# Two MLPs behind window attention: the first MLP's activation as Relu and Square on ScalarE and one max/min on VectorE

## The chip, the cores and the metric

One core of one Trainium2 chip. The time is the device time of one execution in microseconds; three executions of the kernel before took 999.17, 999.47 and 1000.1 us, median 999.47. Engines by the profile's names: PE is TensorE (PEld its weight loads), DVE VectorE, ACT ScalarE, POOL GpSimd, SP SyncE, which issues the DMAs.

## What is computed

Attention with a window of 128 keys over 4 batches, 8 heads, 576 positions and heads of 64 columns, then two MLPs on the 2304 tokens of 512 columns, each with 2048 hidden columns:

```python
h = x @ w_in                                  # first MLP
neg = h <= -1.0
pos = h >= 1.0
g = np.where(pos, h, np.where(neg, 0.0, (h + 1.0) ** 2 / 4.0))
x = g @ w_out
h = x @ w_in2                                 # second MLP
g = h * np.clip(h + 3.0, 0.0, 6.0) / 6.0
out = g @ w_out2
```

## The kernel before

All products keep fp32 accuracy: an operand is split into a high part in fp32r and the rest, and a product is three matmuls (low times high, high times low, high times high).

The tokens of the first MLP come in seven blocks: three of 256 and four of 384. A block runs over 16 chunks of the hidden columns (f). Per chunk, `first` (L549) makes h in one PSUM bank with twelve matmuls; `activate` (L578 to L580) makes r from it, ScalarE casts r to the high part of g (L137), GpSimd subtracts for the low part (L144; VectorE in the last block), and two chunks later `second` (L591) multiplies g by w_out with twelve matmuls. h alternates between two banks in the first three blocks and in the last one; in the blocks between, from the first wide one on, it has one bank (`h0`), so that the next chunk's matmuls wait until L580 has read h.

In the kernel before, the activation is max(h, square(min(max(h, -1), 1)/2 + 1/2)):

- L578, VectorE: r = min(max(h, -1), 1), h from PSUM
- L579, ScalarE: r = Square(0.5 r + 0.5)
- L580, VectorE: r = max(h, r), h from PSUM again

Attention is run in between. For each head and block of queries there is a step: scores on TensorE (L329), bias and row minimum on VectorE (L350), Exp on ScalarE (L353), for most heads a sum, reciprocal and scaling (L356, L357 on VectorE, L358 on GpSimd), transposes on TensorE (L380, L381), their split (L137 ScalarE, L393 VectorE) and the product with v (L466, or L411 in the first units). L303 and L305 split k, L141 casts v on whichever engine the scheduler picks (`nc.any`). A hook after each chunk issues attention's steps and the conversion of the weights of w_in and w_out, which arrive as fp64 words (L178 and L179 on ScalarE, L185 to L189 on VectorE, then a split by L137 and L144, operations of 128 x 1024).

The last block of the first MLP has no attention beside it; there the second MLP's weights are converted (names with `wb`, `mb`, `rawb`). The second MLP activates with L635 (ScalarE, Relu from PSUM, immediately scaled and biased) and L636 (VectorE, min and multiply in one operation).

The order on each engine is not the program's: the framework's scheduler simulates the program with its own costs and orders every engine's instructions by it (except SP's, which keep the program's order). An engine runs its instructions strictly in that order. So other operations in `activate` give another order around them.

Of the kernel before, what the change touches and what calls it, by code (L numbers as in the profile page):

```python
# [14 lines left out]
AF = mybir.ActivationFunctionType  # L15
ALU = mybir.AluOpType
# [22 lines left out]
def tile_window_attention_two_mlps(  # L39
# [15 lines left out]
    nc = tc.nc  # L55
# [7 lines left out]
    scale = 1.0 / math.sqrt(D)  # L63
# [71 lines left out]
    def split_hi(eng, hi, x):  # L135
        if eng == "act":
            nc.scalar.copy(hi, x)  # L137
        elif eng == "pool":
            nc.gpsimd.tensor_scalar(out=hi, in0=x, scalar1=1.0, scalar2=1.0, op0=ALU.mult, op1=ALU.mult)
        else:  # L140
            engines[eng].tensor_copy(hi, x)  # L141

    def split_lo(eng, lo, x, hi):
        engines[eng].tensor_tensor(out=lo, in0=x, in1=hi.bitcast(F32), op=ALU.subtract)  # L144
# [417 lines left out]
    class Mlp1(Mlp):  # L562
# [11 lines left out]
        def activate(self, ps, n):  # L574


            r, g = self.tiles()
            nc.vector.tensor_scalar(out=r[:, :n], in0=ps[:, :n], scalar1=-1.0, scalar2=1.0, op0=ALU.max, op1=ALU.min)  # L578
            nc.scalar.activation(out=r[:, :n], in_=r[:, :n], func=AF.Square, bias=0.5, scale=0.5)  # L579
            nc.vector.tensor_tensor(out=r[:, :n], in0=ps[:, :n], in1=r[:, :n], op=ALU.max)  # L580
            split_hi(HI["g"], g[:, 0, :n], r[:, :n])
            split_lo(LO[self.g_lo], g[:, 1, :n], r[:, :n], g[:, 0, :n])
            return g
# [305 lines left out]
```

## Time and profile before

| | |
|---|---|
| median of three executions | 999.47 us |
| span of the profiled execution | 997.9 us |
| execution time around that span | not recorded apart; the three executions lie 1.3 to 2.2 us above it |
| PE, PEld busy | 968.9, 882.8 us |
| DVE, ACT, POOL busy | 602.9, 515.9, 259.3 us |
| instructions on DVE, ACT, POOL | 1544, 1260, 403 |

The span goes from the first to the last instruction on the chip. TensorE is busy 97% of it, and its granted clock is 0.85 of full speed from 25 to 50 us and 1.00 from 50 us on. The first 50 us are loads and attention alone, then attention and the first MLP run together to about 525 us, the first MLP's last block to about 600, and the second MLP to the end.

### The profile page before, as it was taken

What the parts mean: (1) busy time and instruction counts of PE and PEld (TensorE: products, weight loads), DVE (VectorE), ACT (ScalarE), POOL (GpSimd) and SP (SyncE); (2) the same over time, 40 slices, a digit from 0 to 9 for tenths busy, and PEclk for the clock granted to TensorE, in tenths of its full rate; (3) what the DMA queues carried; (4) which work ended last, traced back from release to release, by engine and by line L of the source; (5) the groups of instructions that cost most, each with busy time, mean ns of one, the idle gap of its engine ahead of it and who ended that gap; (6) DMA issues with size and microseconds to landing.
All of it is one profiled execution on the core that took longest, in us unless ns stands there. A gap on an engine that the chain in (4) does not pass through costs nothing.

```text
span 997.9 us, 16828 instructions
## 1 busy us (share of the span) xinstructions
PE 968.9 (97%) x5748; PEld 882.8 (88%) x5748; DVE 602.9 (60%) x1544; ACT 515.9 (52%) x1260; POOL 259.3 (26%) x403
## 2 busy tenths in 40 slices
PE   7799999999999999999999999999999999999998
PEld 5687888999999998899999999999988888888886
DVE  4889996587678666668764998942242224223222
ACT  5688874567657566656653878522242223222121
POOL 3335454456545555455530000000000000000000
PEclk9899999999999999999999999999999999999999
DMA  5685823223212121222203884000030002001001
GB/s 171 168 258 173 271 66 87 78 67 94 75 42 80 50 80 44 63 59 80 62 12 105 293 277 169 1 1 1 1 106 1 1 1 84 1 1 43 1 1 42
DMA packets 75092, 80.00 MB, mean 80 GB/s; under 512 B 8704, under 2 KB 67072, under 8 KB 75008
## 3 DMA queue, kind: packets, MB, share of 16 engines
q1 hardware_dynamic: 75008, 78.94, 25.8%
q8 instruction: 45, 0.74, 0.3%
q14 instruction: 39, 0.32, 0.1%
HBM read 68.42 MB, written 10.49 MB: 79 GB/s over the span
## 4 chain that ended last, share of the span: by engine, by line
PE 85%; DVE 6%; ACT 4%; issue 2%; DMA 2%; POOL 1%; SPq 0%; ACTq 0%; DVEq 0%; POOLq 0%
PE h L549 37%; PE acc L646 20%; PE acc L591 17%; PE s L329 3%; PE r L466 3%; PE r L411 2%; PE t L380 1%; PE t L381 1%; DVE kl L305 1%; DVE r L578 1%; DMA qr<-qT 1%; ACT p L353 1%; DVE r L580 1%; DVE p L350 1%; DMA vr<-v 1%
## 5 line engine op out<-in xcount | busy, mean ns | idle before, releaser
L549 PE MATMUL h<-x,wa 128*128 128x384 f32 (+1 forms) x1344 | 231.5, 316 | 4.4 <-DVE r L580 2.5
L591 PE MATMUL acc<-g,wa 128*128 128x384 f32 (+1 forms) x1344 | 228.8, 315 | 1.7 <-POOL g L144 1.5
L549 PEld LDWEIGHTS h<-x,wa 128*128 128x128 f32 x1344 | 207.6, 190 | 7.0 <-DVE r L580 4.4
L549 PE MATMUL h<-x,wb 128*128 128x512 f32 (+1 forms) x960 | 210.5, 368 | 0.0
L591 PEld LDWEIGHTS acc<-g,wa 128*128 128x128 f32 x1344 | 206.3, 189 | 4.0 <-POOL g L144 2.2
L646 PE MATMUL acc<-wb,g 128*128 128x512 f32 x864 | 209.4, 390 | 0.0
L549 PEld LDWEIGHTS h<-x,wb 128*128 128x128 f32 x960 | 176.3, 188 | 25.0
L646 PEld LDWEIGHTS acc<-wb,g 128*128 128x128 f32 x864 | 161.7, 188 | 32.3
L636 DVE SCALAR_TENSOR_TENSOR r<-r,h 128x512 f32<-128x512 f32 (+1 forms) x80 | 50.7, 633 | 195.5 <-ACT r L635 195.4
L635 ACT ACTIVATE r<-h 128x512 f32<-128x512 f32 (+1 forms) x80 | 44.4, 556 | 207.9 <-PE h L549 207.8
L137 ACT CAST g<-r 128x384 fp32r<-128x384 f32 (+2 forms) x192 | 98.3, 512 | 69.6 <-DVE r L636 48.7
L144 POOL TENSOR_TENSOR g<-r,g 128x256 fp32r<-128x256 f32 (+1 forms) x96 | 92.0, 958 | 129.2 <-ACT g L137 114.0
L579 ACT ACTIVATE r<-r 128x384 f32<-128x384 f32 (+1 forms) x112 | 53.6, 478 | 93.5 <-DVE r L578 93.3
L353 ACT ACTIVATE p<-p,sm 128x256 f32<-128x256 f32 (+2 forms) x160 | 76.0, 476 | 24.4 <-DVE sm L350 21.6
L144 DVE TENSOR_TENSOR g<-r,g 128x384 fp32r<-128x384 f32 (+1 forms) x96 | 59.9, 624 | 44.7 <-ACT g L137 44.6
L578 DVE TENSOR_SCALAR r<-h 128x384 f32<-128x384 f32 (+1 forms) x112 | 55.5, 496 | 37.4 <-PE h L549 33.2
L144 POOL TENSOR_TENSOR qs<-qr,qs 64x256 fp32r<-64x256 f32 (+3 forms) x88 | 68.8, 781 | 28.4 <-issue 7.5
L580 DVE TENSOR_TENSOR r<-h,r 128x384 f32<-128x384 f32 (+1 forms) x112 | 55.7, 497 | 28.9 <-ACT r L579 28.3
L350 DVE CUSTOM_DVE_ANT_0 p<-s,dist 128x256 f32<-128x256 f32 (+2 forms) x160 | 59.7, 375 | 11.1 <-PE s L329 8.8
L358 POOL TENSOR_SCALAR p<-p,sm 128x256 f32<-128x256 f32 (+1 forms) x104 | 48.1, 463 | 61.7 <-DVE sm L357 37.4
L329 PE MATMUL s<-kh,qs 128*128 128x256 f32 (+2 forms) x160 | 55.0, 347 | 1.8 <-POOL qs L144 1.2
L305 DVE SCALAR_TENSOR_TENSOR kl<-kr,kh 128x256 fp32r<-128x256 f32 (+4 forms) x88 | 51.7, 587 | 7.3 <-ACT kh L303 7.1
(75 smaller groups left out, 1153.5 us busy)
## 6 DMA issues: line engine op xcount, KB each, us to landing
rawa<-w_in SPq DMA_DIRECT2D x16, 512.0 KB, 5.6
rawa<-w_out SPq DMA_DIRECT2D x16, 512.0 KB, 5.1
rawb<-w_in SPq DMA_DIRECT2D x16, 512.0 KB, 3.8
rawb<-w_out SPq DMA_DIRECT2D x16, 512.0 KB, 4.6
kr<-kT SPq DMA_DIRECT2D x80, 64.0 KB, 2.3
out<-o SPq DMA_DIRECT2D x18, 256.0 KB, 2.1
qr<-qT SPq DMA_DIRECT2D x64, 64.0 KB, 2.3
vr<-v SPq DMA_DIRECT2D x24, 128.0 KB, 2.4
```

The source lines that it names most:

```text
L137: nc.scalar.copy(hi, x)
L144: engines[eng].tensor_tensor(out=lo, in0=x, in1=hi.bitcast(F32), op=ALU.subtract)
L305: nc.vector.scalar_tensor_tensor(out=u.kl[:, :nk], in0=u.kr[:, :nk], scalar=unit, in1=u.kh[:, :nk].bitcast(F32), op0=ALU.mult, op1=ALU.sub ...
L329: nc.tensor.matmul(ps[:m, :nk], q[:, qo:qo + m], k[:, ko:ko + nk], start=(w == 0), stop=(w == len(parts) - 1))
L350: nc.vector.tensor_tensor_reduce(out=pt[:m, :nk], in0=ps[:m, :nk], in1=dist[:m, bo:bo + nk], scale=-slopes[u.h], scalar=3.0e38, op0=ALU.ad ...
L353: nc.scalar.activation(out=pt[:m, :nk], in_=pt[:m, :nk], func=AF.Exp, bias=sm[:m, 0:1], scale=-1.0, accum_out=None if u.whole else sm[:m, ...
L549: nc.tensor.matmul(ps[:, :n], self.W.w_in(a, c, f), self.x_chunk(x, b, c, n), start=(k == 0), stop=(k == 3 * KC - 1))
L578: nc.vector.tensor_scalar(out=r[:, :n], in0=ps[:, :n], scalar1=-1.0, scalar2=1.0, op0=ALU.max, op1=ALU.min)
L579: nc.scalar.activation(out=r[:, :n], in_=r[:, :n], func=AF.Square, bias=0.5, scale=0.5)
L580: nc.vector.tensor_tensor(out=r[:, :n], in0=ps[:, :n], in1=r[:, :n], op=ALU.max)
L591: nc.tensor.matmul(acc[i][:, o * n:(o + 1) * n], self.W.w_out(a, f)[:, e * P:(e + 1) * P], g[:, b, :n], start=(first and k == 0 and o == 0 ...
L646: nc.tensor.matmul(acc[t][:, :DM], g[:, b, t * P:(t + 1) * P], self.W.w_out(a, f), start=(first and k == 0), stop=(last and k == 2))
```

## The change

The activation is computed as min(max(h, 1), square(relu(h/2 + 1/2))). For h >= 1 the square is at least h, so the minimum is h; for h <= -1 the Relu gives 0; between, the square is at most 1. Relu from PSUM and Square are ScalarE operations, maximum and minimum are one VectorE operation with two inputs.

```diff
             r, g = self.tiles()
-            nc.vector.tensor_scalar(out=r[:, :n], in0=ps[:, :n], scalar1=-1.0, scalar2=1.0, op0=ALU.max, op1=ALU.min)
-            nc.scalar.activation(out=r[:, :n], in_=r[:, :n], func=AF.Square, bias=0.5, scale=0.5)
-            nc.vector.tensor_tensor(out=r[:, :n], in0=ps[:, :n], in1=r[:, :n], op=ALU.max)
+            nc.scalar.activation(out=r[:, :n], in_=ps[:, :n], func=AF.Relu, bias=0.5, scale=0.5)
+            nc.scalar.activation(out=r[:, :n], in_=r[:, :n], func=AF.Square)
+            nc.vector.scalar_tensor_tensor(out=r[:, :n], in0=ps[:, :n], scalar=1.0, in1=r[:, :n],
+                                           op0=ALU.max, op1=ALU.min)
             split_hi(HI["g"], g[:, 0, :n], r[:, :n])
```

In the changed kernel L578 is the Relu, L579 the Square, L580 the VectorE operation; lines behind it are one higher.

The order of the instructions, at two places. First ScalarE between 50 and 150 us (p, sm: attention's probabilities and row values; th: transposed probabilities; wa, ma, rawa: a weight in conversion; r, g: the activation). Before:

```order
L353 ACTIVATE p12_1_958<-p12_1_958,sm12_1_959 128x256
L178 ACTIVATE ma5_1027<-rawa5_771 128x1024
L137 CAST wa4_1024<-ma4_893 128x1024
L353 ACTIVATE p12_2_995<-p12_2_995,sm12_2_996 64x192
L579 ACTIVATE r_1012<-r_1012 128x256
L179 ACTIVATE rawa5_771<-rawa5_771 128x1024
L137 CAST x_76<-x11_1030 128x256
L137 COPY th12_972<-t12_1_1041 128x256
L137 CAST g_1013<-r_1012 128x256
```

The Square is the activation's only operation on ScalarE, with two Exps ahead of it. The same place on ScalarE now:

```order
L137 COPY th12_972<-t12_0_973 128x256
L578 ACTIVATE r_1012<-h_999 128x256
L137 CAST wa4_1024<-ma4_893 128x1024
L353 ACTIVATE p12_1_958<-p12_1_958,sm12_1_959 128x256
L579 ACTIVATE r_1012<-r_1012 128x256
L178 ACTIVATE ma5_1027<-rawa5_771 128x1024
L179 ACTIVATE rawa5_771<-rawa5_771 128x1024
L353 ACTIVATE p12_2_995<-p12_2_995,sm12_2_996 64x192
L137 CAST g_1013<-r_1012 128x256
```

The Relu of h_999 stands ahead of the Exp of p12_1, which it followed as Square; a weight's cast (L137 wa4) and that Exp stand between Relu and Square.

Second, a wide block near 457 us, with h in one bank (kl: low part of k; x: attention's output; sm: row sums). VectorE before:

```order
L144 TENSOR_TENSOR x_76<-xf72_6990,x_76 128x256
L305 SCALAR_TENSOR_TENSOR kl77_7169<-kr77_6968,kh77_7168 128x384
L356 TENSOR_SCALAR sm75_1_7106<-sm75_1_7106 128x1
L357 RECIPROCAL sm75_1_7106<-sm75_1_7106 128x1
L578 TENSOR_SCALAR r_7125<-h_7112 128x384
L580 TENSOR_TENSOR r_7125<-h_7112,r_7125 128x384
L350 ISA p76_0_7161,sm76_0_7162<-s76_0_7158,dist_95 128x256
```

L578 and L580 stand together behind the softmax's L357. ScalarE at that activation now:

```order
L137 CAST qs77_7170<-qr77_6969 128x256
L353 ACTIVATE p75_1_7105,sm75_1_7106<-p75_1_7105,sm75_1_7106 128x256
L578 ACTIVATE r_7125<-h_7112 128x384
L579 ACTIVATE r_7125<-r_7125 128x384
L137 CAST g_7126<-r_7125 128x384
L137 CAST th75_7151<-t75_0_7153 128x256
L353 ACTIVATE p76_0_7161,sm76_0_7162<-p76_0_7161,sm76_0_7162 128x256
```

Relu and Square follow the Exp of p75_1 without anything between. VectorE there now:

```order
L144 TENSOR_TENSOR x_76<-xf72_6990,x_76 128x256
L305 SCALAR_TENSOR_TENSOR kl77_7169<-kr77_6968,kh77_7168 128x384
L356 TENSOR_SCALAR sm75_1_7106<-sm75_1_7106 128x1
L357 RECIPROCAL sm75_1_7106<-sm75_1_7106 128x1
L580 SCALAR_TENSOR_TENSOR r_7125<-h_7112,r_7125 128x384
L350 ISA p76_0_7161,sm76_0_7162<-s76_0_7158,dist_95 128x256
```

L578 has left VectorE's queue and L580 keeps its place behind L357. Everything else there stands in the order of before.

## Rows read from the trace of the kernel before

**Rows 1.** Busy time by stage; us, then PE, PEld, DVE, ACT, POOL, clock, DMA:
```profile
50.00:150.00 100.00, 96.19 (x738) 84.68 (x738) 93.69 (x225) 83.10 (x193) 48.70 (x49) 1.00 0.61 192
150.00:300.00 150.00, 146.66 (x1141) 143.63 (x1141) 108.16 (x367) 92.47 (x285) 75.90 (x126) 1.00 0.27 73
300.00:525.00 225.00, 218.41 (x1387) 212.53 (x1386) 160.27 (x563) 136.49 (x440) 115.74 (x196) 1.00 0.22 59
550.00:600.00 50.00, 50.00 (x290) 50.00 (x289) 47.27 (x71) 40.84 (x58) 0.00 (x0) 1.00 0.83 284
```

**Rows 2.** Waits, whole span: who waited for whom, us in total, times, longest:
```profile
ACT r L579 <- DVE r L578: 93.3, 79, 2.8
...
DVE r L578 <- PE h L549: 33.2, 36, 2.5
...
DVE r L580 <- ACT r L579: 28.3, 64, 0.7
...
PEld h L549 <- DVE r L580: 4.4, 5, 1.2
...
PE h L549 <- DVE r L580: 2.5, 4, 0.9
...
PE t L380 <- DVE sm L356: 2.4, 3, 1.1
PE t L381 <- DVE sm L356: 2.4, 4, 0.8
```

**Rows 3.** Chain that ended last: shares by line, 150 to 300 us, then 300 to 525:
```profile
by line: PE h L549 30.8%; PE acc L591 29.5%; PE r L466 5.9%; PE s L329 4.8%; issue 3.2%; DVE r L578 2.7%; PE t L380 2.4%; DVE r L580 2.4%; PE t L381 2.1%; ACT r L579 2.0%; DMA vr<-v 1.7%; DVE kl L305 1.4%; DVE vs L141 1.0%; DVE xf L484 1.0%
...
by line: PE h L549 30.4%; PE acc L591 29.2%; PE r L466 7.4%; PE s L329 5.0%; PE t L380 2.9%; DVE kl L305 2.7%; PE t L381 2.6%; issue 2.3%; DVE r L578 1.7%; DMA vr<-v 1.7%; DVE tl L393 1.6%; DVE x L144 1.5%; ACT r L579 1.3%; DVE r L580 1.2%;
```

**Rows 4.** Groups by shape: line engine op out<-in shapes xcount | busy us, mean ns | idle before:
```profile
L580 DVE TENSOR_TENSOR r<-h,r 128x384 f32<-128x384 f32 x64 | 35.6, 556 | 19.7 <-ACT r L579 19.3
L578 DVE TENSOR_SCALAR r<-h 128x384 f32<-128x384 f32 x64 | 35.5, 554 | 27.2 <-PE h L549 23.1 <-PE t L381 2.6 <-POOL qs L144 0.6
...
L579 ACT ACTIVATE r<-r 128x384 f32<-128x384 f32 x64 | 33.6, 525 | 69.3 <-DVE r L578 69.3
...
L305 DVE SCALAR_TENSOR_TENSOR kl<-kr,kh 128x256 fp32r<-128x256 f32 x40 | 21.2, 529 | 6.1 <-ACT kh L303 6.0
...
L580 DVE TENSOR_TENSOR r<-h,r 128x256 f32<-128x256 f32 x48 | 20.1, 419 | 9.1 <-ACT r L579 9.0
L578 DVE TENSOR_SCALAR r<-h 128x256 f32<-128x256 f32 x48 | 20.1, 418 | 10.2 <-PE h L549 10.1
L579 ACT ACTIVATE r<-r 128x256 f32<-128x256 f32 x48 | 19.9, 416 | 24.2 <-DVE r L578 24.0
...
L636 DVE SCALAR_TENSOR_TENSOR r<-r,h 128x384 f32<-128x384 f32 x32 | 17.7, 553 | 45.1 <-ACT r L635 45.0
...
L635 ACT ACTIVATE r<-h 128x384 f32<-128x384 f32 x32 | 15.7, 491 | 54.3 <-PE h L549 54.2
```

**Rows 5.** Timeline of one activation, 456 to 460 us; start us, us, what:
```profile
456.13 2.25 PE L591 MATMUL acc<-g,wa 128*128 128x384 f32 x12
...
456.52 1.10 DVE L305 SCALAR_TENSOR_TENSOR kl<-kr,kh 128x384 fp32r<-128x384 f32 x1
456.72 0.19 ACT L353 ACTIVATION_READ_ACCUMULATOR p<-p,sm 128x1 f32 x1
...
457.80 0.54 DVE L578 TENSOR_SCALAR r<-h 128x384 f32<-128x384 f32 x1
...
458.43 0.52 ACT L579 ACTIVATE r<-r 128x384 f32<-128x384 f32 x1 [1.53 <-DVE r L578]
...
458.99 0.56 DVE L580 TENSOR_TENSOR r<-h,r 128x384 f32<-128x384 f32 x1 [0.65 <-ACT r L579]
...
459.60 0.61 PE L549 MATMUL h<-x,wa 128*128 128x384 f32 x2 [0.57 <-DVE r L580]
```

**Rows 6.** Groups, 50 to 150 us, line L578:
```profile
L578 DVE TENSOR_SCALAR r<-h 128x256 f32<-128x256 f32 x18 | 7.4, 411 | 1.8 <-PE h L549 1.7
```

## Prediction

> **What bounds the kernel now.** The views were read in this order: busy time by stage, waits, the chain of work that ended last, durations by shape, and a timeline of one place. The stages [rows 1] show where other engines can cost TensorE anything. From 550 to 600 us, the end of the first MLP without attention, TensorE is busy 50.00 of 50 us: it is the bound, and what the others save there buys nothing. In the three stretches before it TensorE is busy 96.19 of 100, 146.66 of 150 and 218.41 of 225 us, which is 13.7 us of open idle, and by the profile's own note a busy TensorE is not one at its peak. From 50 to 150 us VectorE is busy 93.69 of 100 and ScalarE 83.10: VectorE is nearly full there. From 150 to 525 us neither is (VectorE 72% and 71%, ScalarE 62% and 61%).
>
> The waits [rows 2] name the activation. TensorE's matmuls of h wait for L580 2.5 us in 4 places, its weight loads 4.4 us in 5; these are two views of much the same stalls, because L580 is the last reader of h's bank. TensorE's transposes wait for L356 of the softmax 4.8 us (2.4 at L380, 2.4 at L381). VectorE stands 28.3 us at L580 waiting for the Square between its two operations, and ScalarE 93.3 us at the Square waiting for L578. The chain [rows 3] passes through the three operations for 2.7 + 2.4 + 2.0 = 7.1% of 150 us (10.7 us), then for 1.7 + 1.3 + 1.2 = 4.2% of 225 us (9.5 us): some 20 us in all. The other 80% or so of the chain is TensorE and attention, which the change leaves alone.
>
> **The change, part by part.** *VectorE loses* L578: 64 of 554 ns and 48 of 418 ns, 35.5 + 20.1 = 55.6 us [rows 4]. L580 gets a second operation. At 384 columns the second MLP has that form, 553 ns against L580's 556, so nothing changes; at 256 the trace has only L305's form from two SBUF operands, 529 ns against 419. The bounds are 0 and 48 x 110 ns = 5.3 us; I take 0, since L636 is the nearer row (one operand in PSUM).
>
> *ScalarE gains* the Relu: at 384 columns L635 is the same operation, 491 ns, 31.4 us for 64. At 256 from PSUM there is no row. The upper bound is the Square from SBUF, 416 ns; the lower takes from L635 what the Square loses from 384 to 256 columns (525 - 416 = 109 ns): 382 ns. For 48 that is 18.3 to 20.0 us; I take 18.3, as PSUM is the nearer source, and 50 us in all. The Square keeps its 525 and 416 ns.
>
> By these rows the Relu is 63 ns shorter on ScalarE than the max/min on VectorE that it replaces. The Trainium skill, ScalarE: Activation LUTs, Rules for kernel authors, says the opposite: relu, max and min belong on VectorE, which can be up to about three times as fast per element; its reason is a fast mode in bf16, and these operands are fp32 with h in PSUM, where the rows show no such advantage. By the formula of that page (What ACT_TABLE_LOAD costs), 186 ns + 0.833 ns an element, the 112 Relus would be an estimated 51.6 us.
>
> *The casts that the scheduler places freely* follow the load: the order shows seven casts of v fewer on VectorE and seven more on ScalarE. At the price of a Relu, which is an upper bound (their shapes are smaller), that is 7 x 0.49 = 3.4 us spread over 375 us; I take nothing. Matmuls, DMAs and GpSimd's operations are the same in number.
>
> *Per activation* the path from h's last matmul to the free bank was 554 + 525 + 556 ns with two changes of engine, and becomes 491 + 525 + 553 with one: 66 ns less by durations. Over 20 us of chain that is 4%, 0.8 us. The larger part is the queue ahead of the first operation. The timeline [rows 5] shows it: ScalarE has finished the Exp of L353 and its read at 456.91 us; TensorE has begun the next matmuls (L591) at 456.13, so h is complete soon after; but L578 starts only at 457.80, behind L305 on VectorE. The Square ends at 458.95, L580 at 459.55, and TensorE has stood idle 0.57 us (its loads 0.78). In the changed order the same neighbours stand there, and the Relu and the Square come right behind the Exp on ScalarE: they could end near 457.95, VectorE is free by then (L578 starts at 457.80 now), and the bank would be free near 458.5, a whole microsecond earlier. That stall goes. What is late next is TensorE's own queue of attention matmuls.
>
> *From 150 to 525 us* I therefore price the stalls on the bank, between 2.5 and 4.4 us [rows 2], at 3 us of gain. Below lies the case that the transposes' 4.8 us go too, as L356 no longer stands behind L578: up to 9.2. Above: ScalarE's Exp now stands behind a Relu that waits for h, as it stood behind a Square that waited for L578; this can be worth nothing or eat the 3 us.
>
> *From 50 to 150 us* 18 activations move [rows 6]. VectorE falls from 93.7 by 7.4 to 86.3, ScalarE rises from 83.1 by 18 x 0.382 = 6.9 (7.5 with the upper price) to 90.0 to 90.6. If the busiest queue set the time, the gain would be 93.7 - 90.6 = 3.1 us. The bounds are wider: all 7.4 if VectorE's work alone sets it and its 6.3 us of idle stays, and a loss of 7.5 if ScalarE's present 16.9 us of idle are all waits on others that cannot be filled. I take half of the 3.1: 1.5 us, because in the new order ScalarE runs one to four other operations between Relu and Square in 14 of the first 16 activations, so the latency won elsewhere isn't won here.
>
> *From 550 to 600 us* twelve of 0.49 us take ScalarE from 40.84 to 46.7 of 50, twelve of 0.554 take VectorE from 47.27 to 40.6 [rows 1, 4]. The two swap roles, TensorE covers both (two banks for h again), price 0. If that cover went, ScalarE above 50 of 50 would be the sign; it would take 3.3 us more.
>
> The sum is -3 - 1.5 = -4.5 us. The profiled execution has a span of 997.9 us, so the new span would be 993.4; the runs' median stands 1.6 above that span at 999.5, which gives **995.0 us**.
>
> **The rivals.** *Only the full stretch gains.* From 150 us on VectorE is at 71%, and each Relu may find as long a queue on ScalarE (60%, rising to about 70%) as L578 found on VectorE. Against it stands the place in rows 5. Then only the 1.5 us remain: 998.0. The Trainium skill, Perfetto Trace Analysis, Optimizing Scalar/DVE Operations, advises the move to ScalarE where VectorE is saturated; by that the first stretch alone would pay, as here.
>
> *Nothing.* The stalls move to another wait, most likely the transposes' on Exp: 999.5.
>
> *Slower: ScalarE's queue becomes the bound of the first 100 us.* The Relu is the head of an in-order queue and waits for the last of h's twelve matmuls, which are scattered between attention's there; behind it stand the Exps that TensorE's transposes need. VectorE waited for h before L578 33.2 us in 112 activations, 0.30 each [rows 2]. VectorE's lead to lose is 93.7 - 90.6 = 3.1 us: from 0.17 us of wait for each of the 18 Relus, ScalarE is the fuller queue and the gain there is gone. At the bound, +7.5 with the 3 us of the later stretch kept: 999.5 + 7.5 - 3 = 1004.0. For it speaks the new order (a weight cast between Relu and Square); against it ScalarE's 16.9 us of idle.
>
> *More.* The whole 3.1, 4.4 and half of the 4.8: -9.9, 989.6.
>
> That Relu and Square need another table of functions would be the change not doing what it says at no cost; both, and Exp, run in the present program, so I give it nothing.
>
> **How the numbers follow.** A measurement of this kernel can tell about 0.2%, 2 us, from no change: faster is below 997.5, slower above 1001.5. The forecast (992 to 997.5) gets 0.44, more (988 to 992) 0.14, only the full stretch 0.14, nothing 0.10, slower 0.18. So faster is 0.58, same 0.24, slower 0.18. The range goes from 988, beyond the larger gain, to 1001.5; it leaves out the slower rival and the last of the gain, 0.20. The forecast's own range is 992 to 997.5.
>
> **What would show it.** Right: VectorE's total falls by some 55 us and ScalarE's rises by some 50; Relu 491 ns at 384, 380 to 416 at 256; L580 within 5 ns at 384; the waits of h on L580 below 1.5 us for matmuls; TensorE 50 of 50 at the end of the first MLP. The first stretch shows ScalarE as the busier one, with TensorE a little fuller. Wrong: h's waits on L580 as before, or transposes that wait for L353 or its casts several microseconds longer; the first MLP's matmuls starting later than now; or ScalarE idle before L578 on h for more than 0.17 us each before 150 us.

## The result, and the profile of the changed kernel

The changed kernel takes 1008.87 us (median of five executions, 1008.15 to 1009.72), the kernel before 999.80 beside it (five, 999.17 to 1001.01). The ratio is 1.0075 with a 95% interval of 1.0051 to 1.0098: slower, where 995.0 was forecast, and outside the range. The profiled execution is the one of 1008.15 us, with a span of 1006.3 against 997.9.

The page of the changed kernel, busy times and TensorE's clock in 40 slices:

```profile
PE 975.9 (97%) x5748; PEld 890.9 (89%) x5748; DVE 557.8 (55%) x1425; ACT 561.1 (56%) x1379; POOL 259.2 (26%) x403
...
PEclk9889899999999999999999999999999999999999
```

VectorE's total fell by 45.1 us and ScalarE's rose by 45.2. The page counts a moment in which two operations of an engine overlap once; added up one by one, their durations fall by 55.3 and rise by 52.0 us, as forecast. The shapes, which answer [rows 4]:

```profile
L580 DVE SCALAR_TENSOR_TENSOR r<-h,r 128x384 f32<-128x384 f32 x64 | 35.6, 557 | 46.9 <-ACT r L579 45.1 <-POOL vs L144 1.0
...
L579 ACT ACTIVATE r<-r 128x384 f32<-128x384 f32 x64 | 33.7, 527 | 1.4
...
L578 ACT ACTIVATE r<-h 128x384 f32<-128x384 f32 x64 | 31.3, 490 | 48.4 <-PE h L549 47.0 <-POOL p L358 1.0 <-POOL qs L144 0.4
...
L580 DVE SCALAR_TENSOR_TENSOR r<-h,r 128x256 f32<-128x256 f32 x48 | 20.2, 421 | 24.6 <-ACT r L579 22.0 <-POOL qs L144 0.7 <-ACT th L137 0.7
...
L578 ACT ACTIVATE r<-h 128x256 f32<-128x256 f32 x48 | 18.2, 379 | 15.2 <-PE h L549 14.3 <-POOL qs L144 0.3 <-POOL vs L144 0.3
```

Every price is within 3 ns of the one that was taken: 490 for the Relu at 384 columns (491 taken), 379 at 256 (382), 557 and 421 for L580. The work that moved is what was said: 55.5 us off VectorE (L578), 49.5 us onto ScalarE. So the loss is no instruction that costs more. Busy time by stage, the columns and stretches of [rows 1]:

```profile
50.00:150.00 100.00, 91.80 (x636) 80.13 (x636) 81.12 (x186) 79.91 (x186) 40.06 (x41) 0.90 0.57 180
150.00:300.00 150.00, 148.59 (x1190) 146.40 (x1189) 98.30 (x327) 108.61 (x331) 80.27 (x125) 1.00 0.29 78
300.00:525.00 225.00, 219.59 (x1390) 214.12 (x1389) 142.12 (x532) 157.23 (x491) 118.03 (x201) 0.99 0.23 61
550.00:600.00 50.00, 50.00 (x291) 50.00 (x290) 43.41 (x59) 43.31 (x67) 0.00 (x0) 1.00 0.83 283
```

From 150 us on the picture is the forecast's: TensorE fuller, and 50.00 of 50 at the end. In the first row everything falls at once. TensorE has 102 fewer matmuls recorded in those 100 us (636 for 738), VectorE and ScalarE are both less busy than before (81.12 for 93.69, 79.91 for 83.10), and the granted clock is 0.90 where it was 1.00. One point of the program dates the loss, the matmuls of h of the 17th chunk. Before, in the timeline:

```profile
135.40 0.76 PE L549 MATMUL h<-x,wa 128*128 128x256 f32 x5
```

The same matmuls in the changed kernel:

```profile
148.91 1.36 PE L549 MATMUL h<-x,wa 128*128 128x256 f32 x10
```

That is 13.5 us late. The last L578 starts at 602.8 us against 595.1, 7.7 us late: 5.8 us are won back between the two places.

Waits over the whole span, for [rows 2]:

```profile
DVE r L580 <- ACT r L579: 67.1, 62, 3.7
ACT r L578 <- PE h L549: 61.3, 62, 3.3
...
PE t L380 <- DVE sm L356: 2.8, 4, 1.0
...
PE t L381 <- DVE sm L356: 2.5, 4, 1.1
...
PE h L549 <- DVE r L580: 0.2, 1, 0.2
```

and the chain's shares by line from 150 to 300 and from 300 to 525 us, for [rows 3]:

```profile
by line: PE h L549 37.1%; PE acc L592 35.0%; PE r L466 6.3%; PE s L329 5.6%; PE t L380 2.9%; PE t L381 2.6%; PE r L411 1.0%; issue 1.0%; DVE r L580 1.0%; ACT r L579 0.9%; DVE ma L189 0.9%; DVE wa L144 0.8%; DVE ma L185 0.7%; ACT wa L137 0.7
...
by line: PE h L549 34.6%; PE acc L592 32.9%; PE r L466 8.5%; PE s L329 6.5%; PE t L380 3.4%; PE t L381 3.1%; DVE x L144 1.9%; DVE kl L305 1.2%; DVE tl L393 1.1%; issue 1.0%; DVE p L350 0.7%; DVE r L580 0.7%; DVE vs L141 0.7%; DVE xf L484 0.
```

TensorE's matmuls of h wait for L580 0.2 us where it was 2.5. The three activation lines' share of the chain fell from 7.1% to 1.9%, and from 4.2% to the 0.7% that the second line names. The transposes wait for L356 as long as before, 5.3 us for 4.8. The activation of [rows 5] in the changed timeline:

```profile
465.37 2.24 PE L592 MATMUL acc<-g,wa 128*128 128x384 f32 x12
...
465.69 1.10 DVE L305 SCALAR_TENSOR_TENSOR kl<-kr,kh 128x384 fp32r<-128x384 f32 x1
465.88 0.19 ACT L353 ACTIVATION_READ_ACCUMULATOR p<-p,sm 128x1 f32 x1
465.98 0.47 ACT L578 ACTIVATE r<-h 128x384 f32<-128x384 f32 x1
466.48 0.53 ACT L579 ACTIVATE r<-r 128x384 f32<-128x384 f32 x1
...
467.04 0.56 DVE L580 SCALAR_TENSOR_TENSOR r<-h,r 128x384 f32<-128x384 f32 x1
```

Relu and Square run straight behind the Exp while VectorE is in L305. L580 ends at 467.60, 2.23 us after the start of TensorE's matmuls of `second`; before, that was 459.55 - 456.13 = 3.42 us. The stall of 0.57 us is gone, as the prediction worked out.

**Where the first 100 us went.** Slices of 25 us from 50 us on, changed kernel (before, the clock is 1.00 in each):

```profile
50.00:75.00 25.00, 22.59 (x150) 19.23 (x149) 15.16 (x42) 16.19 (x41) 8.47 (x9) 0.86 0.70 218
75.00:100.00 25.00, 21.24 (x150) 17.79 (x150) 23.85 (x53) 23.03 (x51) 8.56 (x11) 0.95 0.57 184
100.00:125.00 25.00, 24.76 (x167) 21.58 (x165) 20.09 (x51) 20.11 (x50) 10.31 (x10) 0.85 0.60 185
125.00:150.00 25.00, 23.20 (x174) 21.53 (x175) 22.03 (x42) 20.59 (x47) 12.72 (x12) 0.93 0.42 134
```

The clock is short of 1.00 by 0.14, 0.05, 0.15 and 0.07 of 25 us: 10.25 us of TensorE's work, or 20.5 us spent at half clock. That it is the half shows in single matmuls of h between 50 and 150 us (min, median, max in ns; first and last start). Before:

```profile
L549 PE MATMUL h<-x,wa x216: 277/283/387, 50.8 to 149.3; 128*128 128x256 f32 x108
```

Changed:

```profile
L549 PE MATMUL h<-x,wa x178: 277/283/580, 51.0 to 150.0; 128*128 128x256 f32 x178
```

The longest take 580 ns, twice the median: 1.2 GHz and not 2.4.

The first fall, in slices of 4 us, changed kernel:

```profile
62.00:66.00 4.00, 2.07 (x14) 1.39 (x13) 2.69 (x3) 2.53 (x8) 3.22 (x2) 1.00 0.83 287
66.00:70.00 4.00, 3.73 (x18) 3.22 (x18) 0.43 (x2) 1.19 (x4) 1.53 (x3) 0.59 0.18 50
70.00:74.00 4.00, 4.00 (x21) 3.66 (x21) 2.79 (x8) 0.69 (x3) 0.00 (x0) 0.56 0.21 62
```

The same slices of the kernel before:

```profile
62.00:66.00 4.00, 4.00 (x29) 3.35 (x29) 4.00 (x6) 2.61 (x9) 2.83 (x3) 1.00 0.89 325
66.00:70.00 4.00, 3.67 (x31) 3.34 (x30) 3.57 (x14) 2.71 (x5) 0.42 (x1) 1.00 0.53 142
70.00:74.00 4.00, 3.49 (x29) 3.03 (x27) 3.63 (x12) 4.00 (x11) 0.78 (x1) 1.00 0.70 200
```

From 62 to 66 us TensorE works 2.07 of 4 us. Then its clock falls, and in the next 8 us it is busy nearly all the time with 39 matmuls where it had 60. The other engines now run dry behind it: VectorE 0.43 of 4 us, ScalarE 1.19. That is why nobody is full in the sums: a slow TensorE looks busy and makes the others look idle. What kept TensorE idle, in the changed timeline:

```profile
61.81 1.21 DVE L144 TENSOR_TENSOR wa<-ma,wa 128x1024 fp32r<-128x1024 f32 x1
...
62.70 2.57 POOL L144 TENSOR_TENSOR g<-r,g 128x256 fp32r<-128x256 f32 x1 [3.65 <-ACT g L137]
...
62.94 0.61 DVE L305 SCALAR_TENSOR_TENSOR kl<-kr,kh 128x448 fp32r<-128x448 f32 x1
...
63.48 1.21 DVE L187 SCALAR_TENSOR_TENSOR ma<-rawa,ma 128x1024 uint32<-128x1024 uint32 x1
...
65.33 0.50 PE L592 MATMUL acc<-g,wa 128*128 128x256 f32 x2 [1.88 <-POOL g L144]
```

and the subtraction that makes g's low part at the same place before:

```profile
63.08 0.74 POOL L144 TENSOR_TENSOR g<-r,g 128x256 fp32r<-128x256 f32 x1 [1.66 <-ACT g L137]
...
63.14 1.16 DVE L305 SCALAR_TENSOR_TENSOR kl<-kr,kh 128x448 fp32r<-128x448 f32 x1
```

GpSimd's subtraction takes 0.74 us before and 2.57 now. It starts inside VectorE's operation on wa and ends 0.58 us behind the last of three VectorE operations without a gap, each with two inputs in SBUF. Before, it started 0.06 us ahead of L305, and L305 was the one stretched, to 1.16 us from 0.61. Three such operations stood without a gap before, too (L187 from 62.00 us, L305, L144 from 64.23 us): what differs is the moment at which ScalarE's cast of g releases the subtraction, at the change from one VectorE operation to the next before, and inside one now. The Trainium skill, SBUF — State Buffer, Who interferes with whom, says that a VectorE instruction with two SBUF inputs and a GpSimd instruction that reads SBUF exclude each other, and that whichever starts first makes the other wait; the two places agree with it, once in either direction. That the wait goes on over three operations in a row, as here, is not in it.

The two later falls before 150 us follow a single wait of TensorE as well. From 74 to 97.4 us and from 108 to 128 us, the stretches that end where the clock falls, the longest are 1.3 us for a weight's low part and 1.8 us for q's low part (qs); before, no wait of TensorE between 50 and 150 us is longer than 0.6 us:

```profile
PE h L549 <- DVE wa L144: 2.0, 3, 1.3
...
PE s L329 <- POOL qs L144: 1.8, 1, 1.8
```

A fall long after that has another cause of the idle time. From 400 to 404 us TensorE is busy 2.95 of 4 us (a transpose waits 1.05 us for the softmax's L356), and then the clock is at its lower level:

```profile
400.00:404.00 4.00, 2.95 (x18) 2.50 (x17) 3.54 (x13) 2.68 (x12) 2.89 (x6) 1.00 0.14 33
404.00:408.00 4.00, 3.99 (x16) 3.87 (x16) 1.89 (x12) 2.16 (x9) 1.44 (x3) 0.58 0.16 39
```

The Trainium skill, TensorE: Matmul & The Clock Gate, What's actually happening, says that TensorE falls back to half its clock when it has not been kept busy, and that activity releases it; all four falls agree in the order of events.

### The profile page after: what moved, and what is told of

Same layout as the page of the kernel before. It is cut to its first block, busy times and chain, and to the rows that moved or that the text cites. A ratio compares the mean times of both kernels' runs of the same rounds, so it can differ in the third digit from the quotient of the medians.

```text
span 1006.3 us, 16790 instructions
## 1 busy us (share of the span) xinstructions
PE 975.9 (97%) x5748; PEld 890.9 (89%) x5748; DVE 557.8 (55%) x1425; ACT 561.1 (56%) x1379; POOL 259.2 (26%) x403
## 4 chain that ended last, share of the span: by engine, by line
PE 88%; ACT 4%; DVE 4%; issue 1%; POOL 1%; DMA 1%; SPq 0%; DVEq 0%; ACTq 0%; POOLq 0%
PE h L549 38%; PE acc L647 20%; PE acc L592 18%; PE s L329 3%; PE r L466 3%; PE r L411 2%; PE t L380 2%; PE t L381 2%; ACT rawa L179 1%; DMA qr<-qT 1%; ACT p L353 1%; DVE ma L189 1%; ACT wa L137 1%; PE s L116 1%; PE busy L116 1%
## 5 line engine op out<-in xcount | busy, mean ns | idle before, releaser
L549 PE MATMUL h<-x,wa 128*128 128x384 f32 (+1 forms) x1344 | 234.5, 320 | 2.2 <-DVE wa L144 2.0
L592 PE MATMUL acc<-g,wa 128*128 128x384 f32 (+1 forms) x1344 | 228.8, 316 | 1.9 <-POOL g L144 1.9
L549 PEld LDWEIGHTS h<-x,wa 128*128 128x128 f32 x1344 | 211.9, 194 | 4.0 <-DVE wa L144 2.6
L592 PEld LDWEIGHTS acc<-g,wa 128*128 128x128 f32 x1344 | 207.8, 190 | 2.9 <-POOL g L144 2.1
L137 ACT CAST g<-r 128x384 fp32r<-128x384 f32 (+2 forms) x192 | 98.3, 512 | 72.4 <-DVE r L637 48.2
L144 POOL TENSOR_TENSOR g<-r,g 128x256 fp32r<-128x256 f32 (+1 forms) x96 | 93.9, 978 | 142.0 <-ACT g L137 111.3
L580 DVE SCALAR_TENSOR_TENSOR r<-h,r 128x384 f32<-128x384 f32 (+1 forms) x112 | 55.8, 499 | 71.5 <-ACT r L579 67.1
L578 ACT ACTIVATE r<-h 128x384 f32<-128x384 f32 (+1 forms) x112 | 49.5, 442 | 63.6 <-PE h L549 61.3
L144 DVE TENSOR_TENSOR g<-r,g 128x384 fp32r<-128x384 f32 (+1 forms) x96 | 59.9, 624 | 45.0 <-ACT g L137 44.9
L144 POOL TENSOR_TENSOR qs<-qr,qs 64x256 fp32r<-64x256 f32 (+3 forms) x88 | 64.3, 731 | 21.5 <-POOL g L144 5.3
L579 ACT ACTIVATE r<-r 128x384 f32<-128x384 f32 (+1 forms) x112 | 53.7, 480 | 2.4
L305 DVE SCALAR_TENSOR_TENSOR kl<-kr,kh 128x256 fp32r<-128x256 f32 (+4 forms) x88 | 50.2, 571 | 6.9 <-ACT kh L303 6.7
```

Of the source, the lines that this page charges most:

```text
L305: nc.vector.scalar_tensor_tensor(out=u.kl[:, :nk], in0=u.kr[:, :nk], scalar=unit, in1=u.kh[:, :nk].bitcast(F32), op0=ALU.mult, op1=ALU.sub ...
L549: nc.tensor.matmul(ps[:, :n], self.W.w_in(a, c, f), self.x_chunk(x, b, c, n), start=(k == 0), stop=(k == 3 * KC - 1))
L580: nc.vector.scalar_tensor_tensor(out=r[:, :n], in0=ps[:, :n], scalar=1.0, in1=r[:, :n], op0=ALU.max, op1=ALU.min)
L592: nc.tensor.matmul(acc[i][:, o * n:(o + 1) * n], self.W.w_out(a, f)[:, e * P:(e + 1) * P], g[:, b, :n], start=(first and k == 0 and o == 0 ...
```

## The experiments

The theory: in the first 16 chunks the changed order leaves TensorE idle for a microsecond or two at a time, its clock falls, and that costs about 10 of the 13 us lost there (10.25 us of work, by the slices above); from the 17th chunk on the change gains as forecast. The first rival is the prediction's own: ScalarE's queue bounds that stretch. The second is that the new form itself costs time wherever it stands. The runs were made in three groups on three chips, and every ratio is against the kernel before in the same group (medians 1001.43, 1000.86 and 1000.67 us). Every edit also lets the scheduler order all engines anew, so no run changes one thing alone. Where one kernel's executions differ, their clock differs with them: the ten of the first experiment lie between 993.9 us (mean clock 0.995) and 1002.7 (0.981).

**1. The change from the 17th chunk on only**, the form of before until then:

```diff
+            if self.n_first > 16:
                 nc.scalar.activation(out=r[:, :n], in_=ps[:, :n], func=AF.Relu, bias=0.5, scale=0.5)
...
+            else:
+                nc.vector.tensor_scalar(out=r[:, :n], in0=ps[:, :n], scalar1=-1.0, scalar2=1.0, op0=ALU.max, op1=ALU.min)
...
```

> The first 16 activations (the two half blocks beside which w_in and w_out are converted) as before, the other 96 as in the change. If the whole loss lies in the first 150 us (the changed kernel's 17th group of h matmuls starts 13.5 us late, its last ends 8.4 us late, so 5 us were won back after), the time is 994 to 996 us and the granted clock stays full from 40 us on. If the loss is made anywhere by ScalarE's longer queue, or if the later gain was only TensorE catching up on work that was late, it is 999 us or more.

Measured: 996.38 us, ratio 0.9961 (0.9937 to 0.9984). The clock is 1.00 from 50 to 150 us. The later 96 activations gain 5 us. The second rival falls here.

**2. The change in the first 16 chunks only**, the other way round:

```diff
+            if self.n_first <= 16:
                 nc.scalar.activation(out=r[:, :n], in_=ps[:, :n], func=AF.Relu, bias=0.5, scale=0.5)
...
```

> The first 16 activations as in the change, the other 96 as before. If the loss lies in the first 150 us: 1011 to 1014 us (999.8 + 13.5, and less if a later stretch takes some up), with stretches at half clock before 150 us. If the early stretch is harmless by itself: 999 to 1001 us.

Measured: 1012.53 us, ratio 1.0112 (1.0081 to 1.0143); clock 0.90 from 50 to 150 us. The whole loss, and 11 us of it, is in the first 16 activations. Neither of the two runs says yet whether ScalarE's queue or the clock does it.

**3. The changed kernel with more zero matmuls.** The kernel has a helper, `keep_busy`, that multiplies zeros into a bank about to be overwritten, ahead of attention's scores. Here it runs at full width (512 columns) in all of the first three units of attention and not only in the first, and ahead of each of the first 16 chunks of h. The result stays the same; TensorE gets more to do.

```diff
-                keep_busy(ps, BANK if u.unit == 0 else 2 * P)
+                keep_busy(ps, BANK)
...
+            if self.keep is False and self.n_first <= 16:
+                keep_busy(ps, BANK)
```

> The changed kernel with more of the matmuls on zeros (512 instead of 256 columns a step in the second and third unit of attention, and 512 columns ahead of each of the first 16 groups of h). If the half clock (some 24 us of it in the changed kernel before 150 us and near 405) makes the loss, and TensorE's activity before it decides, the clock stays full or nearly so and the time falls to 995 to 1001 us. If ScalarE's queue is the bound of the first stretch whatever the clock is, the time stays at 1007 us or above (the added matmuls cost TensorE some 8 us where it is not the bound).

Measured: 1001.15 us (998.0 to 1003.94), ratio 0.9989 (0.9968 to 1.0009). From 50 to 150 us:

```profile
50.00:150.00 100.00, 96.05 (x753) 83.81 (x753) 92.01 (x208) 87.06 (x207) 46.95 (x45) 1.00 0.59 187
```

**4. The kernel before with the same two edits.**

> The kernel before with the same added matmuls: their own cost where the clock is full already. 999 to 1003 us by both theories; the difference to the changed kernel with them is what the change does at full clock (-5 by the clock theory, +5 or more by the queue theory).

Measured: 1005.47 us (1003.3 to 1007.01), ratio 1.0035 (1.0018 to 1.0053), above what was expected; clock 0.98 in that stretch. To the kernel before the added matmuls cost 4 us; to the changed one they bring some 8 (1001.15 for 1008.87, in another group), and the changed kernel's clock no longer falls in that stretch: 1.00 for 0.90. But the order of experiment 3 is another one, too: TensorE's longest wait from 57 to 150 us is 0.9 us there, and the changed kernel's three of 1.3 to 1.9 us are gone. So experiment 3 doesn't tell the clock from the waits that come ahead of its falls. Adding useless work to TensorE makes the kernel faster. A full queue on ScalarE can't be helped by that, and in experiment 3 ScalarE carries more in those 100 us (87.06) than in the changed kernel (79.91). With the clock nearly held in both, the change is worth 1001.15 - 1005.47 = -4.3 us.

**5. The changed kernel with g's low part on VectorE in the first 16 chunks**, so that GpSimd's subtraction can't be held up:

```diff
-            split_lo(LO[self.g_lo], g[:, 1, :n], r[:, :n], g[:, 0, :n])
+            split_lo("dve" if self.n_first <= 16 else LO[self.g_lo], g[:, 1, :n], r[:, :n], g[:, 0, :n])
```

> The changed kernel with the low part of g of the first 16 activations subtracted on VectorE instead of GpSimd. In the changed kernel the first fall of the clock (66.7 us) follows TensorE's 1.9 us wait for such a subtraction that took GpSimd 2.57 instead of 0.73 us beside VectorE's operations on SBUF. If GpSimd's long operations are what starves TensorE there, the half clock before 150 us (20.5 us of it) goes for the most part and the time is 995 to 1000 us, though VectorE has 16 x 0.42 us more. If the starving comes from ScalarE's queue, or from whatever order comes out, the half clock stays and the time is 1005 us or more.

Measured: 995.33 us (993.61 to 1000.89), ratio 0.9936 (0.9908 to 0.9963): faster than both kernels. The profiled execution is the slowest of the ten and has one fall in this stretch (clock 0.82 from 50 to 75 us, 1.00 in the next three slices):

```profile
50.00:150.00 100.00, 96.60 (x713) 84.19 (x714) 87.70 (x221) 87.10 (x211) 28.44 (x31) 0.96 0.60 188
```

Relu and Square are still on ScalarE, which is busier (87.10) than in the changed kernel, and the kernel is 5.5 us faster than before. The prediction's slower rival falls.

**6. The kernel before with fewer zero matmuls**, none outside the first unit:

```diff
-            if u.whole:
-                keep_busy(ps, BANK if u.unit == 0 else 2 * P)
+            if u.unit == 0:
+                keep_busy(ps, BANK)
```

> The kernel before without the matmuls on zeros in the second and third unit of attention: nothing of ScalarE, VectorE or GpSimd changes in number. If a less active TensorE loses its clock there and the clock sets the time, half clock appears between 50 and 150 us and the time rises by about half of it, to 1004 to 1012 us. If the engines beside TensorE set the time of that stretch whatever the clock, it stays within 997 to 1002 us.

Measured: 1010.8 us (1004.74 to 1012.59), ratio 1.0082 (1.0052 to 1.0112). The 35 zero matmuls that the kernel before has between 50 and 150 us, 9.8 us of TensorE's time, are gone, and it is 10 us slower. The profiled execution (1005.48, one of the faster ones) has the clock at 0.85 and 0.93 in the first two slices:

```profile
50.00:75.00 25.00, 22.65 (x150) 19.50 (x149) 19.68 (x52) 17.34 (x40) 8.16 (x9) 0.85 0.67 212
75.00:100.00 25.00, 22.16 (x153) 19.02 (x152) 20.51 (x51) 20.32 (x48) 11.60 (x11) 0.93 0.54 179
```

These rows read like the changed kernel's: about 150 matmuls in each slice, VectorE and ScalarE under 21 of 25 us. The activation of before, untouched, makes a loss of the same size once TensorE has more idle time (7.5 of the 100 us for 3.8) in an order of its own.

**7. The maximum back on VectorE in the first 16 chunks**, in the change's formula:

```diff
+            if self.n_first <= 16:
+                nc.vector.tensor_scalar(out=r[:, :n], in0=ps[:, :n], scalar1=1.0, scalar2=0.0, op0=ALU.add, op1=ALU.max)
+                nc.scalar.activation(out=r[:, :n], in_=r[:, :n], func=AF.Square, scale=0.5)
+            else:
...
```

> The change's formula everywhere, but the Relu of the first 16 activations on VectorE (max(h + 1, 0), then Square of half of it on ScalarE, then the max/min). If where the first operation runs decides, not the formula: as with the early activations unchanged, 994 to 998 us, full clock from 60 us on. If the formula or the new VectorE operation costs something early: 1003 us or more.

Measured: 995.47 us (993.77 to 999.79), ratio 0.9936 (0.9908 to 0.9964); clock 0.99 from 50 to 150 us. It is the engine of the first operation, and the order that comes with it, that matters there, and not the formula or L580's second operation. Experiments 5 and 7 reach the same time by opposite ways: 5 gives VectorE work, 7 leaves it there.

**8. The kernel before with the edit of experiment 5**, to see whether that edit is a gain in itself:

> The kernel before with the low part of g of the first 16 activations on VectorE: the control for the run that did so in the changed kernel (995.3 us). VectorE is busy 93.7 of 100 us in that stretch already and gets 6.7 us more. If that run was fast because the change had made room on VectorE for this, the kernel before gains nothing from it: 1000 to 1006 us. If taking GpSimd out is a gain by itself, with the change or without: 993 to 998 us, and the change is then worth 0 or less beside it.

Measured: 1009.12 us, ratio 1.0067 (1.004 to 1.0095). The edit that brings the changed kernel from 1008.87 to 995.33 makes the kernel before 8.5 us slower, more than either expectation. It is no gain in itself. In the profiled execution the clock is 0.86 from 75 to 100 us and 1.00 in the other three slices, and it falls once more at 167 us: 5.1 us of work, where the span is 10.5 us longer than before (1008.4 for 997.9). The rest is not explained.

**9. The changed kernel again**, beside 8 and 10:

> The changed kernel unaltered, on the chip of these runs. The clock that is granted varies from run to run here (the kernel before: mean 0.982 to 0.995, 1006.6 to 999.0 us). If the changed kernel's loss is its own order and not the luck of five runs: 1006 to 1011 us with a mean clock of 0.979 to 0.985 in nearly all. If its low clock was luck: some runs at 0.99 and more, and those at 999 to 1003 us.

Measured: 1011.25 us, ratio 1.0095 (1.0061 to 1.013); clock 0.85 from 50 to 150 us, for 0.90 in the first profile: a little slower and a little lower in clock than expected. The loss is there on another chip.

**10. One instruction moved.** Of all 112 activations only the third, the one of 62.70 us, gets g's low part from VectorE:

```diff
-            split_lo(LO[self.g_lo], g[:, 1, :n], r[:, :n], g[:, 0, :n])
+            split_lo("dve" if self.n_first == 3 else LO[self.g_lo], g[:, 1, :n], r[:, :n], g[:, 0, :n])
```

> The changed kernel with one instruction moved: the low part of g of the third activation, the 2.57 us GpSimd operation for which TensorE waits 1.88 us at 63.4 us. The order up to 60 us stays. If that wait starts the first fall of the clock (66.7 to 73.5 us), the clock is full from 50 to 75 us, the third to ninth group of h come 4 us or more earlier, and the time is 1000 to 1005 us; the later falls may stay. If TensorE's mean activity in the stretch decides and not one wait: the clock still falls near 67 us, and the time stays at 1006 to 1010 us.

Measured: 1002.4 us (998.28 to 1003.79), ratio 0.9995 (0.9974 to 1.0017). One instruction of 0.4 us is worth some 9 us against experiment 9. The first slice keeps its clock, later ones don't:

```profile
50.00:75.00 25.00, 23.05 (x174) 19.56 (x174) 20.16 (x56) 21.29 (x51) 11.14 (x10) 1.00 0.82 249
75.00:100.00 25.00, 22.49 (x154) 18.99 (x152) 21.38 (x47) 19.77 (x48) 9.99 (x10) 0.90 0.49 161
```

In its timeline GpSimd is held even longer, on another operation, and TensorE goes on with L592, since g's low part no longer stands behind it:

```profile
62.28 4.77 POOL L144 TENSOR_TENSOR qs<-qr,qs 64x320 fp32r<-64x320 f32 x1
...
64.78 0.41 DVE L144 TENSOR_TENSOR g<-r,g 128x256 fp32r<-128x256 f32 x1
```

So a blocked GpSimd cost nothing here, where TensorE had no need to wait for it. GpSimd started before the run of VectorE's two-input operations (63.11 to 66.33 us) and was still the one held up, so starting first did not spare it here as it did in the kernel before (GpSimd's spans are rough). The edit moves the order around it too, so that the clock's later falls differ is not proof of a chain from the first to the next.

**The clock taken out of each profile.** Half of the time at half clock after 50 us, read from the granted clock, is work that TensorE missed: 11.9 us in the changed kernel, none in the kernel before. Taken from the span of each profiled execution, this leaves 997.9 us for the kernel before, 999.3 for experiment 2 and 998.2 for 6, which keep the late activations of before; with the change there it leaves 994.4 for the changed kernel, 995.4 for its repeat (9), and 993.2, 992.7, 994.5 and 993.8 for 1, 5, 7 and 10. The spans of these nine runs reach from 993.2 to 1012.0 us; what is left falls into two groups, on the average 4.5 us apart, by the form of the late activations. In the first 16 the change costs some 1.3 us beyond the clock (994.4 against 993.2, 999.3 against 997.9). Experiment 8, with 1003.3, is the exception; 3 and 4, with their added matmuls, come to 998.7 and 999.8.

## Why the prediction was wrong

**The step that failed** is the pricing of 50 to 150 us: "If the busiest queue set the time, the gain would be 93.7 - 90.6 = 3.1 us", of which half was taken. It weighed busy times of VectorE and ScalarE and took TensorE's clock of 1.00 as given. From the third chunk's first matmul of h to the 17th's the kernel before needs 135.40 - 50.81 = 84.6 us, the changed one 148.91 - 51.00 = 97.9: +13.3 where -1.5 stood. The clock is the larger part, 10.25 us of work (the four slices above). The smaller part is waits that the new order has: TensorE's idle time in the 100 us rises from 3.8 to 8.2 us, with 1.9 us for g and 2.1 for q's split (qs), for which it waited 0.9 us and not at all before. The clock's 10.25 and the 4.4 us of idle time come to 14.6 us, 1.3 more than the loss, so the split is only that exact. The waits alone were inside the bounds given (-7.4 to +7.5); the clock was in none of them, and no rival priced it. The code and the rows to see it were there: zero matmuls in that stretch, and a TensorE with only 3.8 us idle of 100, so that a wait of 2 us would be a new thing.

**The slower rival** had the side, the stretch and even its sign, and the wrong mechanism. ScalarE stood idle before L578 on h for 4.5 us over the 15 activations recorded from 50 to 150 us, 0.30 each, above the 0.17 that was named as the point. But these are four waits and not fifteen, as the prediction's 33.2 us for 112 activations were 36. One of them is 3.3 us, from 126.6 to 129.9: it begins while TensorE waits for qs and ends inside the third fall of the clock, so the sign came for the most part from TensorE. And ScalarE as a whole was less busy, not fuller, and with 87.1 us of work in experiments 3 and 5 it held nothing up. A sign that a second mechanism also produces decides nothing alone; ScalarE's busy time in the same row was the better one.

**From 150 to 525 us** the mechanism was right: h's waits on L580 fell from 2.5 to 0.2 us for matmuls, and the stall of [rows 5] went as worked out. The size was above the 3 us: 5.8 us between the 17th chunk and the last activation, although the fall at 404 us lies in it, and 5 us in experiment 1. The chain shows two lines that fell and were not priced: "issue", from 3.2% to 1.0% of the 150 us, and L305, from 2.7% to 1.2% of the 225 us, 3.3 and 3.4 us; how much of the surplus they are was not taken apart. The transposes' waits did not go, so the case of 9.2 us was wrong.

**From 550 to 600 us** nothing changed, TensorE 50.00 of 50, as said. VectorE and ScalarE swapped less than worked out (43.4 and 43.3, for 40.6 and 46.7).

**The whole sum of -4.5 us** is near what the change is worth when the clock holds (-4.3 between experiments 3 and 4), but partly by luck. The activations from the 17th chunk on bring 5.0 us by themselves (experiment 1) where 3 were priced, and the first 16 add nothing to that where 1.5 were. It was a sum for a kernel whose first 100 us stay at 2.4 GHz, and the changed order does not do that.

**Open**: why the order of experiment 8 is slow beyond its clock; whether the waits ahead of the falls at 97 and 128 us cause them, which no run moved by themselves; and whether any other change of order would cost the kernel before its clock. With the activation of before it fell in three other orders (4, 6 and 8); with the change's formula on VectorE it hardly did (7).

## What to carry to other kernels

Where TensorE is the bound and its clock is at the upper level only because it is nearly never idle, price a change of order by TensorE's idle time in one place, not by the other engines' busy sums: one wait of 1.9 us was followed by 7 us at half clock, and the changed stretch lost 10 us of work that way in three such falls. Matmuls of zeros in a kernel can be what holds its clock (experiment 6, though the order moved there too): look at TensorE's idle time around them before moving work from one engine to another. When a kernel gets slower and every engine is less busy, read the clock and the number of matmuls a slice first.

## What was not expected of the hardware

- Without the 35 matmuls of zeros between 50 and 150 us, 9.8 us of TensorE's time, the kernel before takes 10 us more: 1010.8 for 1000.86. More of them cost it 4 us and brought the changed one some 8.
- A subtraction of 128 x 256 on GpSimd took 0.74 us or 2.57, and one of 64 x 320 0.86 us or 4.77, the longer time with a run of VectorE's operations on SBUF beside it.
- Relu from PSUM to fp32 in SBUF takes ScalarE 490 ns for 384 columns and 379 for 256; max and min in one took VectorE 554 and 418 for the same.
